# Keys, queries and FFN inputs transposed by DMA within SBUF in a chunk-selecting attention with an FFN behind it

## The chip, the cores and the metric

One Trainium2 chip, one core, one launch. The time is the device time of the launch in microseconds, as the median of several runs. A separate execution was taken with the hardware profiler; its lines are the ones that are read here, and its own time stands beside them.

## The reference

Four sequences (B) of 768 positions, eight heads of 64, float32 in and out. Keys are cut into 24 chunks of 32. For each query an upper bound of its scores with each chunk is worked out from the chunk's per-dimension minimum and maximum; the six best chunks that are not in the future are kept, and attention runs over the kept chunks with the causal mask. The result, heads side by side, is the input (3072 tokens of 512) of a two-layer FFN with a squared relu.

```
k_min, k_max = k_chunks.min(axis=3), k_chunks.max(axis=3)       # 24 chunks of 32
ub = sum_d max(q * k_min, q * k_max)                            # bound per query and chunk
top = the 6 chunks with the highest ub, future chunks left out
scores = where(chunk selected and causal, q @ k.T / 8, -1e9)
x = softmax(scores) @ v          -> (B * S, H * D) = (3072, 512)
h = relu(x @ w_in)               -> (3072, 2048)
out = (h * h) @ w_out            -> (3072, 512)
```

## The kernel before

The kernel is written as a list of operations (`plan.op`, line 60). Each has a table of engines that may do it with a planned cost in microseconds, a due number, the operations that it needs, and the buffers that it holds. `Plan.order` (line 70) simulates them greedily: of all that can start, it takes the engine with the earliest start, and among that engine's operations within 0.06 us the one with the lowest due number. The instructions are then written in order of planned start, so each engine's queue has that order for good. Hand-over times between engines are planned with `HAND_OVER`; a TensorE operation that starts before `WARM` (14.0 us) is planned at twice its cost; a load's landing is planned by its packets at 0.98 ns each, loads are issued in the order in which the program lists them, and at most eight are under way. Buffers come from pools with a fixed number of slots (`slots`), and an operation whose buffer has no free slot is planned after the one that frees it.

**Loads.** GpSimd issues all loads from HBM, casting float32 to bfloat16. The first 128 positions of all four sequences come as `firsts` (k, q) and `vfirst`, the other 640 as `nat[nm, b]` with tags `kn`, `qn`, `vn`: for sequence 0 by head pair (`load_pair`, line 321), for the others by tiles of 128 positions and all heads (`load_tile`, line 314), keys first, then queries, then values. Three sequences' worth of buffers (`B - 1`) lets the loads run far ahead. GpSimd also does some of the causal masks on the diagonal (line 578), in the same queue.

**Stage A** (`stage_a`) prepares a pair of heads (16 pairs `p`, four per sequence). Six matmuls against the identity turn the key tiles into `kT` in PSUM (`turn_keys`, line 218 by its helper), five turn the query tiles into `qT`. `kT` is copied twice into `kqs` (ScalarE line 213 or VectorE line 215) and reduced twice by VectorE to chunk maxima and minima (`kr`, line 522). `qT` is copied twice into `qss` and split by VectorE into `qp` and `qm` (line 532). TensorE forms the bounds `ub`, VectorE picks with MAX8 (line 502), and the selection is turned (`sT`) and copied below the queries in `qss`, so that the score matmul adds a large negative number to chunks not chosen.

**Stage B** (`stage_b`) does, per head, five banks of 512 scores (`ps`, line 598), the exponential on ScalarE (line 620), the diagonal mask, the products with the values (`av`, line 609) and the normalising into `x` (line 460).

**The FFN** (`ffn`) runs once for the first 128 rows of all sequences (`x_first`) and once per sequence for the other 640. `turn` transposes a tile of 128 rows by four matmuls into PSUM (`xt`) and a copy puts it into `xT`; `up` (line 678) computes 128 hidden features for a range of columns, relu on ScalarE (line 685) or VectorE (line 687) and a square on VectorE (line 696); `down` (line 708) sums over the hidden features and an output store leaves on SP's queue (line 721). For the sequences the ups go in two ranges of 320 columns, with the tiles 0 to 2 turned before the first range and 3 and 4 before the second. The FFN of sequence b is due among the attention of sequence b + 1, and the last one stands alone at the end.

SP's queue holds seven copies of constant rows at the start and the 24 output stores.

Of the kernel before, what the change touches and what calls it, by code (L numbers as in the profile page):

```python
# [11 lines left out]
AX = mybir.AxisListType  # L12
ALU = mybir.AluOpType
ACT = mybir.ActivationFunctionType
# [18 lines left out]
class Op:  # L33
    def __init__(self, where, due, fn, needs, tiles, packets):
        self.where, self.due, self.fn = where, due, fn
        self.needs, self.tiles, self.packets = needs, tiles, packets
        self.engine = None
        self.start = self.end = None


class Plan:
# [10 lines left out]
    WARM = 14.0  # L52
# [7 lines left out]
    def op(self, where, due, fn, needs=(), tiles=(), packets=0):  # L60
        op = Op(where, due, fn, [n for n in needs if n is not None],
                [t for t in tiles if t is not None], packets)
        for t in op.tiles:
            t.users.append(op)
        self.ops.append(op)
        if packets:
            self.loads.append(op)
        return op

    def order(self):  # L70
# [12 lines left out]
        while ready:  # L83
# [36 lines left out]
            op.engine, op.start, op.end = engine, st, st + cost  # L120
            free[engine] = op.end
# [30 lines left out]
def kernel(  # L152
# [9 lines left out]
    nc = tc.nc  # L162

    B, H, S, D = q.shape
    CH = 32
# [22 lines left out]
    ld = ctx.enter_context(tc.tile_pool(name="ld", bufs=B - 1))  # L188
    work = ctx.enter_context(tc.tile_pool(name="work", bufs=2))
# [9 lines left out]
                 "ob": 3, "kn": B - 1, "qn": B - 1, "vn": B - 1, "x": 2, "xT": 2,  # L199
                 "kr": 2, "qp": 2, "qm": 2, "ubm": 2, "m8": 2, "rc": 2})  # L200
    POOLS = {"tp": pst, "ps": pss, "av": psav, "ff": psf, "e": epool, "h2": hpool,
             "ht": hpool, "ob": opool, "kn": ld, "qn": ld, "vn": ld}
# [97 lines left out]
    for b in range(B):  # L300
        for nm in "kqv":
            nat[nm, b] = buffer(nm + "n", [128, NS, H, VW if nm == "v" else D])

    def ones(b, due):
        def go(engine):
            e = nc.vector if engine == "DVE" else nc.gpsimd
            e.memset(nat["v", b].tile[:, :, :, D:D + 1].rearrange(
                "p j h o -> p (j h) o"), 1.0)

        made["ones", b] = plan.op({"DVE": 0.12, "POOL": 0.3}, due, go,  # L310
                                  tiles=[nat["v", b]])

# [61 lines left out]
    for b in range(1, B):  # L374
        ones(b, 20 * NP * b - 70)
        for i, nm in enumerate("kqv"):
            for j in range(1, NT):
                load_tile(nm, b, j, 20 * NP * b - 70 + 5 * i + j)
# [90 lines left out]
    def stage_a(p):  # L469
# [4 lines left out]
        kT = buffer("tp", [128, S], name="kT")  # L474
        qT = buffer("tp" if p else "ps", [128, QC], name="qT")
# [5 lines left out]
        sT = buffer("ps", [128, NT // 2, 128], name="sT")  # L481

# [25 lines left out]
        def copy_selection(e, hh, i):  # L508
# [6 lines left out]
        t = op({"PE": 0.34}, t0, turn_keys,  # L515
               loads_of("k", b, hp) + [made["ident"]], [kT, nat["k", b]])
        late = 4 if p == 0 else 0
        kc = [op({"DVE": 0.475, "ACT": 0.74}, t0 + 3 + hh + late, lambda e, hh=hh: copy(
            e, kqs[0:D, s, hh], kT[D * hh:D * hh + D]),
            [t] + before, [kT]) for hh in range(2)]  # L520
        r = [op({"DVE": 0.86}, t0 + 5 + 2 * mm, lambda _, mm=mm, f=f:
                nc.vector.tensor_reduce(  # L522
                    kr[:, mm], kT.tile.rearrange("d (c j) -> d c j", j=CH),
                    axis=AX.X, op=f), [t], [kT, kr])
             for mm, f in ((0, ALU.max), (1, ALU.min))]
# [4 lines left out]
        t = op({"PE": 0.28}, t0 + 8, turn_queries,  # L530
               loads_of("q", b, hp, False) + [made["ident"]], [qT, nat["q", b]])
        sq = [op({"DVE": 0.40}, t0 + 10 + i, lambda _, d=d, f=f: f(  # L532
            d.tile, qT.tile, 0.0), [t], [qT, d])
            for i, (d, f) in enumerate(((qp, nc.vector.tensor_scalar_max),
                                        (qm, nc.vector.tensor_scalar_min)))]
        qc = [op({"ACT": 0.63, "DVE": 0.40}, t0 + 13 + hh, lambda e, hh=hh: copy(
            e, qss[0:D, s, hh], qT[D * hh:D * hh + D]),
            [t] + before, [qT]) for hh in range(2)]
# [100 lines left out]
    def ffn(x, ready, rows, parts, due, rate, up_tags=("ff", "ff")):  # L639

        n = len(rows)
        xT = buffer("xT", [128, NKI, 128 * n])
# [7 lines left out]
        turned = []  # L650

        def turn(t):
            pt = buffer("ff", [128, NKI, 128], name="xt")

            def go(_):
                for ki in range(NKI):
                    transpose(pt[:, ki], x[:, t, 128 * ki:128 * (ki + 1)])

            op = plan.op({"PE": 0.225}, step(0.225), go, ready(t), [pt] + xs)
            turned.append(plan.op(  # L660
                {"DVE": 0.36, "ACT": 0.54}, at[0] + 0.5,
                lambda e: copy(e, xT[:, :, 128 * t:128 * (t + 1)], pt.tile),
                [op], [pt, xT]))
# [4 lines left out]
        def up(f, c0, c1, i):  # L668
# [7 lines left out]
            def go(_):  # L676
                for ki in range(NKI):
                    nc.tensor.matmul(  # L678
                        ph.tile, lhsT=w_in_sb[:, ki, 128 * f:128 * (f + 1)],
                        rhs=xT[:, ki, c0:c1],  # L680
                        start=(ki == 0), stop=(ki == NKI - 1))

            def relu(e):
                if e == "ACT":
                    nc.scalar.activation(ht.tile, ph.tile, ACT.Relu)  # L685
                else:
# [4 lines left out]
                         turned[c0 // 128:-(-c1 // 128)] + loaded["in", f // 4],  # L691
# [43 lines left out]
    turn, up, down = ffn(x_first, lambda t: x_done[t, 0], first_rows, None,  # L735
# [13 lines left out]
    for b in range(B):  # L749
        x = buffer("x", [128, NS, d_model])  # L750
        x_done[b, 1] = []
        for p in range(NP * b, NP * (b + 1)):
# [5 lines left out]
            None, HALVES * NP * (b + 1) + 10, 2.2, ("ps", "ps") if last else ("ff", "ff"))  # L758
        for c in range(2):
            for t in ((0, 1, 2), (3, 4))[c]:  # L760
                turn(t)
            for f in range(NFI):
                up(f, QC // 2 * c, QC // 2 * (c + 1), f)
# [34 lines left out]
```

## Time and profile before

| | |
|---|---|
| median of 3 runs | 283.24 us (283.13 to 283.76) |
| the profiled execution's own time | 284.56 us |
| its span, first to last instruction | 282.8 us |
| granted TensorE clock | 1.00 |
| HBM read, written | 27.26 MB, 6.29 MB |
| GpSimd's DMA queue | 79,152 packets, 61.9% of 16 engines' span |
| SP's DMA queue | 3,708 packets, 6.3% |

How to read the profile: PE is TensorE's matmuls, PEld its weight loads, DVE VectorE, ACT ScalarE, POOL GpSimd, SP SyncE. Matmuls are pipelined, so the length of one matmul record is longer than the step from one to the next, and a busy PE is not PE at its peak. A group's line gives engine, operation, output and input tiles, shapes, count, busy time and mean length in ns, then the idle time of the engine just before and what ended it. The chain of waits is followed back from the last instruction to whatever released each step. Slices are fortieths of the span, digits are tenths. The time given for a DMA's landing is from issue to completion.

### The profile page before, as it was taken

Reading aid. Unit: us, or ns where it says so; the run is one execution under the profiler, and the core shown is the slowest. Engines: PE = TensorE matmul, PEld = TensorE weight load, DVE = VectorE, ACT = ScalarE, POOL = GpSimd, SP = SyncE. Lnnn points to the kernel's source line nnn. Section 1 sums busy time; section 2 is a strip of 40 time slices with the busy share of each in tenths; the row PEclk is TensorE's granted clock in tenths of the full one; section 3 lists DMA queues with packets and bytes.
Section 4 is the critical chain, followed back from the end, with each engine's and each line's share of the span. In section 5 each row is a group of like instructions: output and inputs, shape, how many; then the busy total and the mean of one; then the engine's idle time right before and its main releaser. Section 6 shows DMA issues by size and latency. Waiting matters only on the chain.

```text
span 282.8 us, 6701 instructions
## 1 busy us (share of the span) xinstructions
PE 265.6 (94%) x2515; PEld 174.2 (62%) x2544; DVE 209.0 (74%) x729; ACT 181.8 (64%) x348; POOL 100.3 (35%) x170
## 2 busy tenths in 40 slices
PE   6778989999999999999999999999999999899994
PEld 2555766566667776565767665667776655567441
DVE  1377999989999999676999996869999612488200
ACT  3265789997896888365868874668688544334111
POOL 8976797699999321000201211002023000000000
PEclk9999999999999999999999999999999999999999
DMA  9999999999999900011000010101000111100021
GB/s 59 183 163 190 146 126 175 178 173 178 171 166 147 81 2 37 12 64 39 37 3 3 0 39 37 41 37 39 1 3 2 38 39 54 57 2 0 37 76 74
DMA packets 82892, 20.61 MB, mean 73 GB/s; under 512 B 75524, under 2 KB 79788, under 8 KB 82860
## 3 DMA queue, kind: packets, MB, share of 16 engines
q0 software_dynamic: 79152, 13.64, 61.9%
q1 hardware_dynamic: 3708, 6.55, 6.3%
q8 instruction: 20, 0.33, 0.5%
q14 instruction: 12, 0.10, 0.1%
HBM read 27.26 MB, written 6.29 MB: 119 GB/s over the span
## 4 chain that ended last, share of the span: by engine, by line
PE 66%; DMA 11%; DVE 10%; POOL 8%; ACT 2%; issue 2%; POOLq 0%; ACTq 0%; DVEq 0%
PE py L708 24%; PE ph L678 24%; PE ps L598 8%; DMA w_out_sb<-in_moe_w_out_dram 6%; PE av L609 4%; DMA k<-in_k_dram 3%; DVE kr L522 2%; DMA qn<-in_q_dram 2%; POOL qn L314 1%; POOL qn L321 1%; POOL kn L321 1%; PE kT L218 1%; PE xt L218 1%; DVE qsc L215 1%; DVE m L502 1%
## 5 line engine op out<-in xcount | busy, mean ns | idle before, releaser
L620 ACT ACTIVATE e<-ps 128x512 bf16<-128x512 f32 x160 | 90.6, 601 | 21.7 <-PE ps L598 19.6
L678 PE MATMUL ph<-xT,w_in_sb 128*128 128x320 bf16 (+2 forms) x605 | 99.8, 303 | 1.5 <-DVE xT L215 0.5
L708 PE MATMUL py<-w_out_sb,h 128*128 128x512 bf16 x358 | 90.2, 379 | 1.2
L678 PEld LDWEIGHTS <-w_in_sb 128*128 128x128 bf16 x608 | 57.9, 98 | 26.5 <-issue 4.0
L578 POOL TENSOR_SCALAR_AFFINE_SELECT e<-e 128x128 bf16<-128x128 bf16 (+1 forms) x74 | 24.9, 339 | 126.0 <-ACT e L620 124.6
L598 PE MATMUL ps<-qsc,kqc 88*128 88x128 bf16 (+1 forms) x320 | 57.7, 272 | 0.5 <-ACT e L620 0.3
L685 ACT ACTIVATE ht<-ph 128x320 bf16<-128x320 f32 (+2 forms) x81 | 35.6, 440 | 28.9 <-PE ph L678 24.2
L708 PEld LDWEIGHTS <-h 128*128 128x128 bf16 x384 | 34.1, 97 | 30.4
L696 DVE TENSOR_TENSOR h<-ht 128x320 bf16<-128x320 bf16 (+2 forms) x152 | 46.0, 323 | 3.4 <-ACT ht L685 3.1
L609 PEld LDWEIGHTS <-e 128*128 128x128 bf16 x640 | 36.9, 97 | 12.8 <-POOL e L578 1.8
L687 DVE TENSOR_SCALAR ht<-ph 128x320 bf16<-128x320 f32 (+2 forms) x71 | 34.8, 490 | 7.0 <-PE ph L678 4.7
L609 PE MATMUL av<-vn,e 128*128 128x65 bf16 x480 | 38.6, 193 | 1.2 <-POOL e L578 0.7
L598 PEld LDWEIGHTS <-kqc 88*128 88x128 bf16 x320 | 25.6, 98 | 11.3 <-issue 1.5
L522 DVE TENSOR_REDUCE kr<-kT 128x24 bf16<-128x768 bf16 x32 | 30.1, 945 | 2.3 <-PE kT L218 2.1
L213 ACT COPY ob<-py 128x512 f32<-128x512 f32 x22 | 12.9, 588 | 27.4 <-PE py L708 27.3
L575 DVE TENSOR_TENSOR e<-e,tri 128x128 bf16<-128x128 bf16 (+1 forms) x54 | 12.8, 239 | 13.1 <-ACT e L620 12.6
L460 DVE TENSOR_TENSOR x<-av,rc 128x320 bf16<-128x320 f32 (+1 forms) x40 | 18.5, 471 | 0.4
L502 DVE MAX8 m<-ubm 128x8 f32<-128x24 f32 x160 | 15.6, 168 | 0.2
L609 PE MATMUL av<-v,e 128*128 128x65 bf16 x160 | 15.2, 193 | 0.1
L213 ACT COPY qsc<-qT 64x640 bf16<-64x640 bf16 x19 | 13.1, 687 | 1.9 <-DVE qm L532 0.7
L215 DVE COPY kqc<-kT 64x768 bf16<-64x768 bf16 x17 | 9.4, 553 | 6.6 <-PE kT L218 6.1
L314 POOL DMA_DIRECT2D qn<-in_q_dram x15 | 13.3, 896 | 2.5 <-DMA w_out_sb<-in_moe_w_out_dram 2.3
(72 smaller groups left out, 272.3 us busy)
## 6 DMA issues: line engine op xcount, KB each, us to landing
out_dram<-ob SPq DMA_DIRECT2D x24, 256.0 KB, 2.0
w_in_sb<-in_moe_w_in_dram POOLq DMA_DIRECT2D x4, 512.0 KB, 9.0
w_out_sb<-in_moe_w_out_dram POOLq DMA_DIRECT2D x4, 512.0 KB, 8.1
kn<-in_k_dram POOLq DMA_DIRECT2D x15, 128.0 KB, 6.5
qn<-in_q_dram POOLq DMA_DIRECT2D x15, 128.0 KB, 6.2
vn<-in_v_dram POOLq DMA_DIRECT2D x15, 128.0 KB, 6.1
kn<-in_k_dram POOLq DMA_DIRECT2D x8, 80.0 KB, 6.7
qn<-in_q_dram POOLq DMA_DIRECT2D x8, 80.0 KB, 6.3
```

The lines of the kernel that those rows point to most:

```text
L213: nc.scalar.copy(dst, src)
L460: return plan.op({"DVE": 0.06 + 0.00108 * D * n}, due, lambda _: nc.vector.tensor_mul(x(), av[:, :, 0:D], rc[:, 0:n].unsqueeze(2).to_broad ...
L522: nc.vector.tensor_reduce(kr[:, mm], kT.tile.rearrange("d (c j) -> d c j", j=CH), axis=AX.X, op=f), [t], [kT, kr])
L578: nc.gpsimd.affine_select(out=e, in_=e, compare_op=ALU.is_ge, fill=0.0, base=0, channel_multiplier=-1, pattern=[[0, n], [1, 128]])
L598: nc.tensor.matmul(ps[:, 128 * c:128 * (c + nt)], lhsT=kqs[:, s, hh, 128 * j:128 * (j + 1)], rhs=qss[:, s, hh, 128 * (t0 - 1):128 * (t0 - ...
L609: nc.tensor.matmul(av[:, t - 1], lhsT=e[:, 128 * c:128 * (c + 1)], rhs=value_tile(b, h, j), start=(i == 0 and c == 0), stop=(i == len(BANK ...
L620: nc.scalar.activation(e.tile, ps.tile, ACT.Exp, scale=scale), [sc], [ps, e])
L678: nc.tensor.matmul(ph.tile, lhsT=w_in_sb[:, ki, 128 * f:128 * (f + 1)], rhs=xT[:, ki, c0:c1], start=(ki == 0), stop=(ki == NKI - 1))
L685: nc.scalar.activation(ht.tile, ph.tile, ACT.Relu)
L687: nc.vector.tensor_scalar_max(ht.tile, ph.tile, 0.0)
L696: {"DVE": 0.06 + w / 1900}, at[0] + 2, lambda _: nc.vector.tensor_mul(h2[f][:, c0:c1], ht.tile, ht.tile), [op], [ht, h2[f]])))
L708: nc.tensor.matmul(py.tile, lhsT=h2[f][:, 128 * t:128 * (t + 1)], rhs=w_out_sb[:, f, :], start=(f == 0), stop=(f == NFI - 1))
```

## The change

Sequence 0 keeps its path. For the sequences 1 to 3 the key and query tiles of 128 positions are loaded by GpSimd into `nt` buffers (six slots, 128 x 512 bf16, one tile each), and SP issues for each a transposing DMA from SBUF to SBUF into `kt` or `qt` (two slots each, four pairs side by side on the free axis). The first key tile is turned the same way from `firsts`. The turns on TensorE for these sequences are gone; copies, reductions and max/min read `kt` and `qt` in SBUF and are planned on VectorE alone. A pair's keys now need the turns of all six tiles of the sequence, and its queries those of all five. The natural `kn` and `qn` buffers shrink to one, for sequence 0.

In the FFN of the sequences 0 to 2, `turn` is the same kind of DMA from `x` into `xT`; the last sequence's and the first rows' stay on TensorE. `xT` has its axes in another order. The ups of each sequence go in ranges of 256 and 384 columns, after two and three tiles.

In the planner `WARM` goes from 14.0 to 23.5, an operation may have a `lag` that delays its result but not its engine, and the costs of a few copies are other numbers. A transposing DMA is planned at 1.2 us on SP with a lag of 1.6.

```diff
-    WARM = 14.0
+    WARM = 23.5
...
-            op.engine, op.start, op.end = engine, st, st + cost
-            free[engine] = op.end
+            op.engine, op.start, op.end = engine, st, st + cost + op.lag
+            free[engine] = st + cost
...
+    ld1 = ctx.enter_context(tc.tile_pool(name="ld1", bufs=1))
+    ldt = ctx.enter_context(tc.tile_pool(name="ldt", bufs=6))
+    tpool = ctx.enter_context(tc.tile_pool(name="tpool", bufs=2))
...
-                 "ob": 3, "kn": B - 1, "qn": B - 1, "vn": B - 1, "x": 2, "xT": 2,
+                 "ob": 3, "kn": 1, "qn": 1, "nt": 6, "kt": 2, "qt": 2,
+                 "vn": B - 1, "x": 2, "xT": 2,
...
+    for b in range(1, B):
+        turned["k", b] = buffer("kt", [128, NT, NP, 128])
+        turned["q", b] = buffer("qt", [128, NS, NP, 128])
+
+    def turn_by_dma(dst, src, due, needs, tiles):
+        return plan.op({"SP": 1.2}, due, lambda _: nc.sync.dma_start_transpose(
+            out=dst(), in_=src()), needs, tiles, lag=1.6)
...
+    def load_turned(nm, b, j, due):
+        dst = turned[nm, b]
+        if j == 0:
+            src, needs = None, loaded[nm, b, "first"]
+        else:
+            src = buffer("nt", [128, H, D])
+            load((nm, b, j), lambda _: nc.gpsimd.dma_start(
+                out=src.tile,
+                in_=SRC[nm][b, :, 128 * j:128 * (j + 1)].rearrange("h p d -> p h d")),
+                due, 1024, [src])
+            needs = loaded[nm, b, j]
+        i = j if nm == "k" else j - 1
+        op = turn_by_dma(
+            lambda: dst[:, i],
+            lambda: (src.tile if src else firsts[nm][:, b]).rearrange(
+                "p h d -> p (h d)"), due, needs, [src, dst])
+        loaded.setdefault((nm, b), []).append(op)
...
-        for i, nm in enumerate("kqv"):
-            for j in range(1, NT):
-                load_tile(nm, b, j, 20 * NP * b - 70 + 5 * i + j)
+        for i, nm in enumerate("kq"):
+            for j in range(0 if nm == "k" else 1, NT):
+                load_turned(nm, b, j, 20 * NP * b - 70 + 5 * i + j)
+        for j in range(1, NT):
+            load_tile("v", b, j, 20 * NP * b - 60 + j)
...
+        if b:
+            kT, qT = turned["k", b], turned["q", b]
+        else:
+            kT = buffer("tp", [128, S], name="kT")
+            qT = buffer("tp" if p else "ps", [128, QC], name="qT")
...
+        def part(t, rows=slice(0, 128)):
+            if b:
+                return t[rows, :, hp]
+            return t[rows].rearrange("d (t j) -> d t j", j=128)
...
-        kc = [op({"DVE": 0.475, "ACT": 0.74}, t0 + 3 + hh + late, lambda e, hh=hh: copy(
-            e, kqs[0:D, s, hh], kT[D * hh:D * hh + D]),
-            [t] + before, [kT]) for hh in range(2)]
+        if b:
+            got = list(loaded["k", b])
+            kc_on, qc_on, q_on = {"DVE": 0.28}, {"DVE": 0.24}, 0.24
+        else:
+            got = [op({"PE": 0.34}, t0, turn_keys, loads_of("k", b, hp) + [made["ident"]],
+                      [kT, nat["k", b]])]
+            kc_on, qc_on = {"DVE": 0.475, "ACT": 0.80}, {"ACT": 0.69, "DVE": 0.41}
+            q_on = 0.40
+        kc = [op(kc_on, t0 + 3 + hh + late, lambda e, hh=hh: copy(
+            e, by_tile(kqs[0:D, s, hh]), part(kT, slice(D * hh, D * hh + D))),
+            got + before, [kT]) for hh in range(2)]
...
-        t = op({"PE": 0.28}, t0 + 8, turn_queries,
-               loads_of("q", b, hp, False) + [made["ident"]], [qT, nat["q", b]])
+        if b:
+            got = list(loaded["q", b])
+        else:
+            got = [op({"PE": 0.28}, t0 + 8, turn_queries,
+                      loads_of("q", b, hp, False) + [made["ident"]], [qT, nat["q", b]])]
...
-        xT = buffer("xT", [128, NKI, 128 * n])
+        xT = buffer("xT", [128, n, NKI, 128])
...
         def turn(t):
+            if by_dma:
+                xt_made.append(turn_by_dma(
+                    lambda: xT[:, t], lambda: x[:, t], step(0.225), ready(t),
+                    [xT] + xs))
+                return
...
-            None, HALVES * NP * (b + 1) + 10, 2.2, ("ps", "ps") if last else ("ff", "ff"))
+            not last, HALVES * NP * (b + 1) + 10, 2.2, ("ps", "ps") if last else ("ff", "ff"))
         for c in range(2):
-            for t in ((0, 1, 2), (3, 4))[c]:
+            tiles = range(2 * c, 2 + (NS - 2) * c)
+            for t in tiles:
                 turn(t)
             for f in range(NFI):
-                up(f, QC // 2 * c, QC // 2 * (c + 1), f)
+                up(f, 128 * tiles[0], 128 * (tiles[-1] + 1), f)
```

## The prediction

> **What bounds the kernel now.** I read the page's busy table and slices first, then the windows by stretch, then the chain of waits, the groups by form, and last GpSimd's timeline and the landing times.
>
> ```profile
> PE 265.6 (94%) x2515; PEld 174.2 (62%) x2544; DVE 209.0 (74%) x729; ACT 181.8 (64%) x348; POOL 100.3 (35%) x170
> DMA  9999999999999900011000010101000111100021
> PE 66%; DMA 11%; DVE 10%; POOL 8%; ACT 2%; issue 2%; POOLq 0%; ACTq 0%; DVEq 0%
> ```
>
> TensorE is busy 94% of the span and carries two thirds of the chain; the DMA engines are full to about 99 us (14 of 40 slices of 7.07 us) and almost idle after. By stretch (columns: length, then PE, PEld, DVE, ACT, POOL busy, granted clock, DMA):
>
> ```profile
> 0.00:20.00 20.00, 13.99 (x99) 8.32 (x100) 8.23 (x31) 8.23 (x12) 17.34 (x25) 1.00 1.68 133
> 20.00:40.00 20.00, 17.86 (x181) 13.31 (x181) 16.67 (x67) 13.22 (x29) 15.26 (x23) 1.00 1.52 155
> 60.00:100.00 40.00, 39.11 (x447) 27.55 (x450) 38.22 (x132) 32.81 (x65) 33.02 (x47) 1.00 1.98 148
> 100.00:140.00 40.00, 39.24 (x403) 25.46 (x404) 31.85 (x110) 28.15 (x54) 4.82 (x15) 1.00 0.09 34
> 140.00:190.00 50.00, 48.85 (x480) 32.47 (x486) 42.51 (x151) 34.21 (x65) 6.81 (x20) 1.00 0.06 23
> 190.00:240.00 50.00, 49.21 (x485) 32.98 (x488) 35.35 (x119) 34.29 (x67) 7.05 (x21) 1.00 0.06 23
> ```
>
> From 60 to 240 us PE is busy 176.4 of 180 us, 98%; its gaps lie before 40 us. Busy is not peak, so I count issue steps from the chain (start, length, what):
>
> ```profile
> 112.52 1.09 PE ph L678 x8
> 118.89 0.86 PE py L708 x4
> 134.60 0.45 PE xt L218 x8
> ```
>
> An FFN column costs 1.09/8/320 = 0.426 ns, a transpose 0.45/8 = 0.056 us. All of PE: FFN 2 x 196,608 columns x 0.423 ns = 166 us; scores 81,920 x 0.425 = 35; 352 transposes x 0.056 = 20; 672 value products x 0.03 = 20; bounds 4; first attention and warm-up 7: 252 of 282.8 us. Of the other 31, about 18 lie before 40 us. From 60 us on PE is the bound; DVE, 96% in 60 to 100, is close behind it there.
>
> **PE transposes removed.** Pairs of sequences 1 to 3: 12 x (6 key + 5 query tiles) = 132. FFN inputs of sequences 0 to 2: 15 x 4 = 60. Together 192 x 0.056 = 10.75 us, all of it between 59.85 us (first key transposes of sequence 1) and 212 us. At 98%: **-10.5 us**. The Trainium skill, page "TensorE: Matmul & The Clock Gate", section "Part 4: PE-mode transpose", puts one transpose at about 275 ns inside a kernel; that would make this 52.8 us. The trace's own record of one is 219 ns long, but eight take 0.45 us: the lengths overlap and only the step comes back.
>
> **Copies.** Per pair, the key and query copies move from PSUM sources on either engine to SBUF sources on VectorE alone:
>
> ```profile
> L215 DVE COPY kqc<-kT 64x768 bf16<-64x768 bf16 x17 | 9.4, 553 | 6.6 <-PE kT L218 6.1
> L213 ACT COPY qsc<-qT 64x640 bf16<-64x640 bf16 x19 | 13.1, 687 | 1.9 <-DVE qm L532 0.7
> L532 DVE TENSOR_SCALAR qp<-qT 128x640 bf16<-128x640 bf16 x16 | 7.8, 485 | 1.0 <-PE qT L218 0.8
> L215 DVE COPY xT<-xt 128x512 bf16<-128x512 bf16 x12 | 4.9, 412 | 3.9 <-PE xt L218 3.8
> ```
>
> ScalarE loses 15/16 x 0.79 + 19/16 x 0.687 = 1.56 us a pair, 18.7 in all, and about 4 of xT. VectorE has 17/16 x 0.553 + 13/16 x 0.483 = 0.98 of copies and 0.97 of max/min a pair. With SBUF sources no row shows these. Lower end: 0.196 (tri from ahead, SBUF to SBUF, 128x128); upper end: today's 0.553 and 0.483. The squaring h<-ht, 128x320 with two SBUF operands at 0.322 against 0.485 for relu from PSUM, is nearest, so I take the change's own plan figures plus the 0.08 by which the trace exceeds the plan today (0.553 against 0.475): 0.36 and 0.32. Then 2 x 0.36 + 4 x 0.32 = 2.0 against 1.95: VectorE gains nothing a pair and loses the xT copies, 3 us. The path gets **0**: PE covers it, and without that cover the upper end is the third rival.
>
> **What SP gains.** 48 transposing DMAs of 128x512: 18 key, 15 query, 15 input tiles. The trace has none. Nearest rows: SP's SBUF-to-SBUF copies of 36 KB, 0.76 us from issue to issue; output stores of 256 KB,
>
> ```profile
> DMA to landing us min/median/max: 2.0/2.0/5.6
> ```
>
> 2.0 us in quiet, 5.6 for the one seen in the full stretch (issued at 59.5); and GpSimd's 128 KB loads, 6.1 to 6.5 us. So an issue costs 0.3 (a store's) to 2 us and a landing 2.0 to 6.5; I take 1.2 an issue (the plan's figure, inside the bounds) and 2.8 in quiet, 5.6 in the full stretch. SP is then occupied 48 x 1.2 = 58 of 280 us. Queued behind a transpose that waits for its tile are output stores (three `ob` buffers, so PE's down results wait only if a store is some 4 us late) and the next transposes.
>
> Against the change stands the Trainium skill, page "VectorE: DVE Perf Modes", section "The three transpose paths": 1309 ns for 128x128 by the DMA crossbar against 390 by TensorE, with the advice to use TensorE where PSUM will do. Four blocks one after the other would be 5.2 us a tile, 251 us for 48, and the slower rival would hold. The trace answers for PE's side, 0.056 us a block, and has no row for the other.
>
> **Sequence 1's start.** This is where the added wait bites:
>
> ```profile
> 45.56 4.41 POOL L314 DMA_DIRECT2D kn<-in_k_dram  x5
> 50.08 0.88 POOL L314 DMA_DIRECT2D qn<-in_q_dram  x1
> 57.14 0.90 POOL L314 DMA_DIRECT2D qn<-in_q_dram  x1
> L218 PE MATMUL qT<-ident,qn x5: 219/219/219, 65.8 to 66.0; 128*128 128x128 bf16 x5
> ```
>
> Today the last query tile is issued at 57.1, lands by about 63.5 and is turned at 65.8; the pair's selection is copied by 73.2 and its scores start at about 75. After: keys land at 52 to 56. The six `nt` slots hold k1 to k5 and q1, so q2 is issued when k1 is turned (52 + 5.6, near 58, today 52.6), q5 near 61; it lands at 67.5 and is turned at 72 to 73. Prepared 7 us later, at 79 to 80: some 4 to 5 late. GpSimd's diagonal masks stand behind the waiting load. Cover: of the first rows' `py` work two groups of 0.86 are left after 76.5 us, and sequence 0's FFN, whose inputs are ready at 75.9, can't start before them (next part). Bounds 0 and +5; I take **+3**, the delay less those two groups. Later sequences have over 20 us in hand.
>
> **FFN inputs.** Normalised at 75.9 and 130.1, first `ph` at 82.1 and about 136.7. Two issues and a landing: 75.9 + 1.2 + 5.6 = 82.7; 130.1 + 1.2 + 2.8 = 134.1. At 134 PE still has `py` and attention to do; at 82 the +3 above already pays for its lack of work: **0** (0 to +1).
>
> **Split 256/384 for 320/320.** Equal columns and counts; relu 0.423 (256) and 0.485 (320) lie on one line: 0. The last FFN, still on PE, starts after two tiles, not three; its first `ph` follows 1.2 us of idle around `xt` at 242 to 244: **-0.5** (0 to -1.3).
>
> **Plan.** WARM 23.5 doubles PE's price up to 23.5 us in the planner, so the order before 40 us changes. The first matmuls are paced by loads (GpSimd 17.3 of 20 us busy): **0**, plus or minus 1. ScalarE's relief and fewer small PE waits could give 0 to -2; taken as 0.
>
> **Sum** against the profiled execution, 284.56 us (span 282.8 and 1.76 around it): 284.56 - 10.5 - 0.5 + 3 = 276.6. The median of the runs, 283.24, is 1.32 lower: 275.2 us. All good ends: 283.24 - 10.5 - 1.3 - 2 - 1 = 268.4. All bad ends: 283.24 - 10.5 + 5 + 1 + 1 = 279.7.
>
> **Rivals.** (1) Slower: the transposing DMA is serial on SP, at s us a tile. Sequence 1's 11 tiles start at 52, so its first pair is ready at 52 + 11s + 7, against 75 needed and 2 us of cover. The gains of 11 us are used up where 52 + 11s + 7 = 75 + 2 + 11, s = 2.6; at s = 4 it is ready at 103, 26 us uncovered, minus 11: 298 us. Beyond 54/16 = 3.4 a sequence's 16 tiles no longer fit its period of some 54 us. For it: engines that are full to 99 us, and 5.6 us for a store. Against: stores at 2.0 in quiet, plain copies at 0.76. (2) Sequence 1 is late by all 5 us, and late FFN inputs and loads behind `nt` on GpSimd add 2 to 3: 278 to 282, say 280. For it: POOL busy 33 of 40 us there. Against: PE's `py` groups. (3) VectorE becomes the bound: if SBUF copies cost as from PSUM, it pays 2 x 0.553 + 4 x 0.483 = 3.04 a pair for 1.95, +13 in all, -3 of xT. In about half of 60 to 240 VectorE is over 93% busy (by stretches of 10 us): +5 there, and in the other half PE gives -5.2; with -0.5 and +3, 285.5. The h row speaks against it.
>
> **Chances.** The sum's case 0.60, rival 2 0.16, rival 3 0.05, rival 1 0.19. A measurement of this kernel can tell about 0.2%, 0.6 us, from no change. Rivals 3 and 1 hold nearly all of slower (0.21) and the no-change case gets 0.03 from the seams: faster 0.76. The range runs from 268.5, the good ends, to 285, which leaves out most of rival 1 and a little of the rest.
>
> **What would show it.** Transposes on `kT`, `qT`, `xt` fall from 272 to 80; 48 transposing DMAs on SP, 1.2 us apart at least, landing in 2.8 us after 100 us and near 5.6 before; the first query maxima of sequence 1 at 72 to 74, not 66.3; PE busy still 97% or more from 100 us on; the last `x` near 230, not 239. Wrong would be: PE idle by microseconds with SP or a DMA as releaser past 100 us, landings over 4 us in quiet, or VectorE copies near 0.5.

## The result: slower by 5.6%, and the profile after

| | before | after |
|---|---|---|
| median of the runs | 283.5 us (4 runs, 283.13 to 284.35) | 299.87 us (4 runs, 297.24 to 301.0) |
| ratio | | 1.056 (95%: 1.048 to 1.064) |
| the profiled execution's own time, span | 284.56, 282.8 us | 301.0, 299.3 us |
| granted TensorE clock over the span | 1.00 | 0.948 |

The forecast was 275.2 us with a range up to 285.0; the median lies 14.9 us above its end. All comparisons below are of medians on the same chip; a number such as "+9.2" is the difference of the two medians in us. The ratios go by the means of the runs, so they can differ a little from the quotient of the medians. The clock's 1.00 before is a little flattering: other executions of the kernel before list 0.98 to 1.00, and the last section shows that its first 20 us were not at full clock.

The page of the changed kernel first: busy time, then slices of 7.5 us, then the chain's shares by engine.

```profile
PE 261.4 (87%) x2329; PEld 165.2 (55%) x2352; DVE 205.0 (69%) x726; ACT 170.4 (57%) x333; POOL 101.5 (34%) x173
...
PEclk9859999977999978999996999999999999999999
DMA  8999999999999999994122000113300011100011
...
PE 43%; DMA 22%; DVE 18%; POOL 9%; issue 3%; SPq 2%; ACT 1%; POOLq 0%; DVEq 0%; ACTq 0%
```

TensorE still does most, but its share of the chain fell from 66% to 43%; DMA and VectorE took it over, and in several slices up to 165 us the granted clock is below full. The span grew by 16.5 us. TensorE's busy time fell by 4.2 us (265.6 to 261.4), so its idle time grew by 20.7 (17.2 to 37.9). Of the 10.75 us of transposes taken out, 6.5 came back as longer busy time. The DMA engines are full for the first 18 slices, to about 135 us; before they were to 99. The last load is issued at 128.6 us, 92.3 before. The stretches (columns as in the prediction: length, busy PE, PEld, DVE, ACT, POOL, granted clock, DMA) show where:

```profile
20.00:40.00 20.00, 17.81 (x201) 13.31 (x199) 16.38 (x68) 14.61 (x33) 15.18 (x23) 0.94 1.78 173
60.00:100.00 40.00, 29.00 (x275) 17.81 (x277) 28.21 (x98) 18.39 (x37) 27.03 (x37) 0.91 1.78 158
100.00:140.00 40.00, 32.40 (x282) 20.04 (x284) 32.90 (x110) 20.98 (x42) 16.78 (x29) 0.91 1.48 123
140.00:190.00 50.00, 46.56 (x429) 30.66 (x431) 45.55 (x153) 32.68 (x65) 6.52 (x20) 0.93 0.11 31
190.00:240.00 50.00, 49.73 (x496) 33.14 (x500) 36.73 (x142) 34.48 (x69) 6.60 (x21) 1.00 0.14 41
...
66.00:68.00 2.00, 2.00 (x11) 1.08 (x10) 0.13 (x1) 0.21 (x1) 2.00 (x3) 0.50 2.31 150
156.00:162.00 6.00, 5.47 (x32) 3.83 (x31) 4.15 (x13) 2.99 (x7) 0.99 (x3) 0.50 0.45 109
```

Between 60 and 140 us TensorE was busy 78.4 of 80 us; now it is busy 61.4, at a lower clock. From 190 to 240 us it is 99.5% busy at full clock: there the change works as meant. The loss thus lies at the start of sequence 1 and in what comes behind it. The chain of waits in that stretch (start, length, what):

```profile
44.05 11.00 DMA nt<-in_k_dram
55.07 1.19 SPq L317
56.35 5.58 DMA kt<-nt
62.02 0.49 POOL nt L335
64.79 0.30 POOL e L635
70.25 8.70 DMA nt<-in_k_dram
78.97 6.55 DMA kt<-nt
90.60 6.53 DMA nt<-in_q_dram
100.13 2.78 SPq L317
102.95 7.80 DMA xT<-x
110.89 1.12 PE ph L739 x3
```

The first key tile lands at 55.05, not 52; turns land and free `nt` slots only by 61.94; GpSimd issues the next query tile at 62.02, and a mask (`e`) stands behind the loads. SP turns ten tiles one after the other, as its timeline shows (start, length of the whole group; the third line is the second line's group without its first turn):

```profile
55.07 7.07 SPq L317 DMA_TRANSPOSE kt<-nt  x5
62.23 9.58 SPq L317 DMA_TRANSPOSE qt<-nt  x5
66.55 5.26 SPq L317 DMA_TRANSPOSE qt<-nt  x4
...
81.81 4.46 SPq L317 DMA_TRANSPOSE kt<-nt  x3
86.55 2.50 SPq L317 DMA_TRANSPOSE xT<-x  x2
89.14 1.28 SPq L317 DMA_TRANSPOSE kt<-nt  x1
...
91.14 7.24 SPq L317 DMA_TRANSPOSE qt<-nt  x5
98.44 5.84 SPq L317 DMA_TRANSPOSE xT<-x  x3
```

Ten turns take 55.07 to 71.81, 1.67 us each on average. In this kernel 3.1 of these us are SP's wait for the second query tile: the first one's turn is issued by 63.45, the next starts at 66.55. The landing times (the last column of the profile's list of DMA issues) are medians of the few landings that the trace tells, seven of the 48:

```profile
kt<-nt SPq DMA_TRANSPOSE x15, 4.8
qt<-nt SPq DMA_TRANSPOSE x15, 6.8
xT<-x SPq DMA_TRANSPOSE x15, 2.4
kt<-k SPq DMA_TRANSPOSE x3, 8.5
```

The first query maxima of sequence 1 come at 78.2 (66.3 before; 72 to 74 was forecast). Further down SP's queue, turns of sequence 2 stand between the tiles of `x`: its five turns begin at 86.55 and end at 104.28. What TensorE does meanwhile, from its timeline (the bracket is the idle time before and its releaser):

```profile
60.91 0.38 PE L655 MATMUL ps<-qsc,kqc 88*128 88x128 bf16 x2
65.16 0.40 PE L666 MATMUL av<-vn,e 128*128 128x65 bf16 x4 [3.87 <-POOL e L635]
65.36 1.90 PE L769 MATMUL py<-w_out_sb,h 128*128 128x512 bf16 x4
...
106.32 0.81 PE L769 MATMUL py<-w_out_sb,h 128*128 128x512 bf16 x3
110.89 1.44 PE L739 MATMUL ph<-xT,w_in_sb 128*128 128x384 bf16 x4 [3.76 <-DMA xT<-x]
```

Behind the first wait four `py` take 1.90 us; the record of four at full clock is 1.03. The clock was 0.50 from 64 to 70 us (the last window above is part of it), and 0.76 in 110 to 120, behind the second wait. The Trainium skill, page "TensorE: Matmul & The Clock Gate", section "Part 1: The HAM clock gate", states that TensorE goes back to half clock after an idle window of about 3.4 us. The two waits, 3.87 and 3.76 us, are of that length, but the clock column falls sooner: at about 63.5, 2.2 us into the first, and within the first us of the second (0.50 from 108 on). It was also 0.50 from 156 to 162 us, behind a wait of only 1.78 us at 153.2, and in the kernel with sequence 1 alone (below) from 63.5 to 66.5, behind one of 2.96. So here the clock fell without a single wait of that length before it.

VectorE's copies, by form (count, busy, mean ns, idle before):

```profile
L220 DVE COPY kqc<-kt 64x768 bf16<-64x768 bf16 x24 | 8.9, 370 | 2.5 <-DMA kt<-nt 2.3
L220 DVE COPY qsc<-qt 64x640 bf16<-64x640 bf16 x24 | 11.4, 477 | 0.2
L589 DVE TENSOR_SCALAR qp<-qt 128x640 bf16<-128x640 bf16 x12 | 5.7, 473 | 3.5 <-issue 3.5
```

The key copies got cheaper (0.553 to 0.370), the query copies and maxima did not.

### The profile page after: what moved, and what is told of

It is laid out like the page before. It is cut to its first block, busy times and chain, and to the rows that moved or that the text cites. A ratio compares the mean times of both kernels' runs of the same rounds, so it can differ in the third digit from the quotient of the medians.

```text
span 299.3 us, 6453 instructions
## 1 busy us (share of the span) xinstructions
PE 261.4 (87%) x2329; PEld 165.2 (55%) x2352; DVE 205.0 (69%) x726; ACT 170.4 (57%) x333; POOL 101.5 (34%) x173
## 4 chain that ended last, share of the span: by engine, by line
PE 43%; DMA 22%; DVE 18%; POOL 9%; issue 3%; SPq 2%; ACT 1%; POOLq 0%; DVEq 0%; ACTq 0%
PE py L769 17%; PE ph L739 16%; DMA nt<-in_k_dram 7%; PE ps L655 5%; DVE kr L575 4%; DMA kt<-nt 4%; DMA kn<-in_k_dram 4%; DMA k<-in_k_dram 3%; PE av L666 3%; DVE h L757 3%; DMA xT<-x 3%; DVE qsc L220 2%; SPq L317 2%; DMA nt<-in_q_dram 2%; DVE ht L748 2%
## 5 line engine op out<-in xcount | busy, mean ns | idle before, releaser
L739 PE MATMUL ph<-xT,w_in_sb 128*128 128x256 bf16 (+2 forms) x608 | 103.5, 309 | 7.5 <-DMA xT<-x 3.8
L769 PE MATMUL py<-w_out_sb,h 128*128 128x512 bf16 x361 | 93.3, 384 | 1.8 <-ACT xT L218 0.5
L746 ACT ACTIVATE ht<-ph 128x384 bf16<-128x384 f32 (+2 forms) x98 | 44.0, 450 | 41.1 <-PE ph L739 32.4
L655 PE MATMUL ps<-qsc,kqc 88*128 88x128 bf16 (+1 forms) x320 | 61.2, 280 | 0.7 <-ACT e L677 0.3
L757 DVE TENSOR_TENSOR h<-ht 128x256 bf16<-128x256 bf16 (+2 forms) x152 | 47.3, 321 | 16.8 <-ACT ht L746 15.9
L748 DVE TENSOR_SCALAR ht<-ph 128x256 bf16<-128x256 f32 (+2 forms) x54 | 25.1, 468 | 4.2 <-PE ph L739 3.6
L575 DVE TENSOR_REDUCE kr<-kt 128x24 bf16<-128x768 bf16 x24 | 22.0, 943 | 0.2
L335 POOL DMA_DIRECT2D nt<-in_q_dram x15 | 13.5, 902 | 11.4 <-DMA kt<-nt 10.0
L335 POOL DMA_DIRECT2D nt<-in_k_dram x15 | 13.4, 918 | 3.9 <-DMA qt<-nt 3.4
L220 DVE COPY qsc<-sT 24x256 bf16<-24x256 bf16 (+1 forms) x36 | 11.4, 318 | 4.6 <-PE sT L223 3.9
```

The costliest lines, as they stand in the source:

```text
L335: load((nm, b, j), lambda _: nc.gpsimd.dma_start(out=src.tile, in_=SRC[nm][b, :, 128 * j:128 * (j + 1)].rearrange("h p d -> p h d")), due, ...
L575: nc.vector.tensor_reduce(kr[:, mm].rearrange("d (t c) -> d t c", c=128 // CH), part(kT).rearrange("d t (c j) -> d t c j", j=CH), axis=AX. ...
L655: nc.tensor.matmul(ps[:, 128 * c:128 * (c + nt)], lhsT=kqs[:, s, hh, 128 * j:128 * (j + 1)], rhs=qss[:, s, hh, 128 * (t0 - 1):128 * (t0 - ...
L739: nc.tensor.matmul(ph.tile, lhsT=w_in_sb[:, ki, 128 * f:128 * (f + 1)], rhs=xT[:, c0 // 128:c1 // 128, ki], start=(ki == 0), stop=(ki == N ...
L748: nc.vector.tensor_scalar_max(ht.tile, ph.tile, 0.0)
L757: {"DVE": 0.06 + w / 1900}, at[0] + 2, lambda _: nc.vector.tensor_mul(h2[f][:, c0:c1], ht.tile, ht.tile), [op], [ht, h2[f]])))
```

## The experiments

The theory after the comparison: sequence 1's start is late because SP turns its tiles in series from a late first landing, and the lateness costs TensorE idle time and clock. The rivals: the `nt` slots hold GpSimd back; GpSimd's masks behind the waiting load; VectorE, which alone may copy now; the FFN inputs; the planner's numbers. All kernels but the first are the changed kernel with the edit shown, and so have `WARM` 23.5 and the ranges 256 and 384; where a sequence goes back to TensorE its natural buffers come back too. Where sequence 1 alone goes by DMA, one `kt` and at most one `qt` slot are left.

**The parts, each alone.** The planner's number, in the kernel before:

```diff
-    WARM = 14.0
+    WARM = 23.5
```

> The kernel before with WARM 23.5 instead of 14.0 and nothing else. Theory A (GpSimd's loads wait for nt slots that a late turn frees, the diagonal masks stand behind them in GpSimd's queue, TensorE idles and its clock falls) and theory B (the turned tiles themselves land too late among the loads, whatever the slots): 282 to 285 us. Theory C (the order that the planner now writes is the worse one): 290 us or more, with PE idle before 60 us.

Measured: 282.94 against 283.83, ratio 0.9965 (0.9948 to 0.9982), -0.9 us. The plan's number is not the loss; it brings a little.

Only the FFN inputs of sequences 0 to 2 (the keys and queries of all sequences on TensorE):

```diff
+    KQ = 4   # sequences from KQ on by DMA: none
-        if b:
+        if b >= KQ:
```

> The change with keys and queries of all sequences on TensorE as before; only the FFN inputs of sequences 0 to 2 are turned by DMA (60 transposes off PE, 3.4 us). Theories A and B: 279 to 283 us, granted clock back at 1.00. If the FFN inputs on SP were a main cost: 290 us or more with PE waiting for xT.

The same, with sequence 0's inputs on TensorE too:

```diff
-            not last, HALVES * NP * (b + 1) + 10, 2.2, ...
+            b in (1, 2), HALVES * NP * (b + 1) + 10, 2.2, ...
```

> Only the FFN inputs of sequences 1 and 2 by DMA (40 transposes off PE, 2.2 us), in the stretch without loads; all keys and queries on TensorE. Theory B: 280 to 282.5 us and no wait of PE on xT. If a turn by DMA costs the path even with quiet engines: 283.5 to 286 us, as with the inputs of all three.

Measured: 284.99 against 283.83, 1.0054 (1.0021 to 1.0086), and 281.93 against 283.77, 0.995 (0.992 to 0.998): +1.2 and -1.8. Sequence 0's five tiles alone make the difference of 3 us, though they take 1.1 us of transposes away. The timeline of TensorE in the first of these two shows the place:

```profile
80.75 1.03 PE L772 MATMUL py<-w_out_sb,h 128*128 128x512 bf16 x4
84.61 0.61 PE L742 MATMUL ph<-xT,w_in_sb 128*128 128x256 bf16 x4 [2.83 <-DMA xT<-x]
```

It waits 2.83 us for the transposing DMA before the FFN of sequence 0, in the stretch in which the loads run.

Only the keys and queries of sequences 1 to 3, then those of sequence 1 alone, then of sequence 1 only the keys:

```diff
-            not last, HALVES * NP * (b + 1) + 10, 2.2, ...
+            b in (), HALVES * NP * (b + 1) + 10, 2.2, ...
...
+    BY_DMA = (1,)   # second and third kernel; all FFN inputs on TensorE in all three
-        if b:
+        if b in BY_DMA:
...
-            got = list(loaded["q", b])  # third: queries turned on TensorE
```

> The change with all FFN inputs on TensorE; only keys and queries of sequences 1 to 3 are turned by DMA (132 transposes off PE, 7.4 us). Theories A and B: 295 to 302 us, nearly the whole loss, with clock below 1 from 60 to 130 us. If the loss needs both halves, because inputs and tiles share SP's queue: below 288 us.

> Only the keys and queries of sequence 1 by DMA; those of 2 and 3 and all FFN inputs on TensorE (44 transposes off PE, 2.5 us). Theory B (sequence 1's tiles come late because SP turns them one after the other from 55 us on and each lands 5 to 8 us later): most of the loss of the keys-and-queries half is here, 289 to 294 us. If the loss is spread over the sequences alike: 284 to 288 us.

> Of sequence 1 the keys alone by DMA, queries on TensorE; all else as before. SP then has 6 turns instead of 11 before the first pair can go on, and the query tiles need no slot. Theory B with SP's serial turning as the cause: the chunk bounds come by 73 to 74 us instead of 78, and the time is 284 to 288 us. If the first landing alone decides: 290 us or more.

| by DMA | ratio (95%) | us |
|---|---|---|
| keys, queries of 1 to 3 | 1.0378 (1.0353 to 1.0403) | +10.7 |
| keys, queries of 1 | 1.0304 (1.0258 to 1.0351) | +9.2 |
| keys of 1 | 1.019 (1.0157 to 1.0222) | +5.3 |

One sequence carries most of the loss. The windows of 60 to 100 us and the query maxima (count, shortest, middle and longest ns, first and last start), first for keys and queries of sequence 1, then for its keys alone:

```profile
60.00:100.00 40.00, 30.94 (x315) 20.00 (x314) 30.32 (x102) 20.03 (x39) 30.07 (x42) 0.96 1.78 147
L593 DVE TENSOR_SCALAR qp<-qt x2: 475/480/486, 77.5 to 80.4; 128x640 bf16<-128x640 bf16 x2
```

```profile
60.00:100.00 40.00, 34.93 (x371) 23.39 (x370) 32.21 (x115) 25.91 (x52) 24.80 (x40) 0.96 1.62 127
L593 DVE TENSOR_SCALAR qp<-qT x2: 468/470/471, 72.3 to 78.2; 128x640 bf16<-128x640 bf16 x2
```

With five turns fewer on SP the first query maxima of sequence 1 start at 72.3 instead of 77.5, TensorE is busy 4 us more of these 40, and the kernel loses 3.9 us less. Of these 5.2 us, 1.8 are an earlier first turn (53.65 against 55.43), and the query tiles need no `nt` slot here either; the next kernel looks at the slots.

**What makes sequence 1 late.** More slots, so that GpSimd needn't wait:

```diff
-    ldt = ctx.enter_context(tc.tile_pool(name="ldt", bufs=6))
+    ldt = ctx.enter_context(tc.tile_pool(name="ldt", bufs=10))
...
-                 "ob": 3, "kn": 1, "qn": 1, "nt": 6, "kt": 2, "qt": 2,
+                 "ob": 3, "kn": 1, "qn": 1, "nt": 10, "kt": 2, "qt": 2,
```

> The change with ten nt slots instead of six, so that the ten key and query tiles of a sequence never wait for a turn of their own sequence. Theory A: q2 to q5 of sequence 1 are issued by 53 us, not 62 to 65, GpSimd does not stop for 10 us, and the time falls to 277 to 287 us. Theory B: landings stay at 5 to 8 us, the first pair of sequence 1 is as late as before, and the time stays at 294 to 301 us.

Measured: 298.17 against 283.83, 1.052 (1.0474 to 1.0567): +14.3, no gain clear of the noise. The timeline of GpSimd has the query loads early again, as in the kernel before, and the tile's view has the turns and their landing:

```profile
56.75 0.90 POOL L335 DMA_DIRECT2D nt<-in_q_dram  x1
```

```profile
L589 DVE TENSOR_SCALAR qp<-qt x12: 448/478/486, 77.7 to 204.2; 128x640 bf16<-128x640 bf16 x12
L317 SPq DMA_TRANSPOSE qt<-nt x15: 1200/1431/3007, 62.4 to 125.4; - x15
...
DMA to landing us min/median/max: 3.9/7.1/7.6
```

The last of these loads is issued at 56.75, yet the first maxima come at 77.7 instead of 78.2: the turns of the queries start at 62.4 as in the changed kernel, take up to 3.0 us each, and land 7.1 us after issue. That load lands 11.9 us after its issue; the same load took 6.2 us before, so turns and loads also slow each other. How much of the lateness that is was not isolated. The slots alone are not what makes sequence 1 late: without their waits, the turns in series and their landings make it as late.

Masks on VectorE only, so that none stands behind a waiting load on GpSimd:

```diff
-                        {"DVE": 0.085 + 0.058 * n, "POOL": 0.15 + 0.13 * n}, due + 1.5,
+                        {"DVE": 0.085 + 0.058 * n}, due + 1.5,
```

> The change with all diagonal masks of the sequences planned on VectorE, none on GpSimd, so that nothing on the way to the values stands behind a load that waits for a slot. Theory A: the 4 us gap of PE at 61 us and those after it vanish and the time is 284 to 291 us. Theory B: the first pair of sequence 1 is as late as before, its query maxima at 77 us or later, and the time is 294 to 301 us.

Measured: 297.95 against 283.77, 1.052 (1.0446 to 1.0594). That mask is the releaser that the trace names for the wait of 3.87 us; without it there the time is much the same, as TensorE waits 6.5 us for the bounds (`ub`) at 72 us instead. Ten slots and the masks on VectorE together were not tried.

A planned landing nearer to the measured one:

```diff
-            out=dst(), in_=src()), needs, tiles, lag=1.6)
+            out=dst(), in_=src()), needs, tiles, lag=5.5)
```

> The change with the planner's lag of a turn 5.5 us instead of 1.6, near the 4.8 to 6.8 us measured among the loads; nothing else. If the order written for early turns is the cause (PE's queue holds work that waits for turns, with other work behind it): 285 to 291 us. Theory B in its strict form (the tiles are late, and there is not enough other work): 293 us or more.

Measured: 295.23 against 283.77, 1.0414 (1.0357 to 1.0472), +11.5 instead of +16.4. The order written for too early a landing costs some 5 us, which may be the same as those of the next part; the rest stays.

**What comes behind the lateness.** The copies of keys and queries allowed on ScalarE again, with the planned prices of VectorE's query copies and maxima raised to 0.40; then, in the plan alone, a pair prepared only after the first scores of the pair two before it (in the changed kernel VectorE's and SP's free time lets the planner pull it ahead); then both:

```diff
-            kc_on, qc_on, q_on = {"DVE": 0.28}, {"DVE": 0.24}, 0.24
+            kc_on, qc_on, q_on = {"DVE": 0.28, "ACT": 0.80}, {"DVE": 0.40, "ACT": 0.69}, 0.40
...
-            got = list(loaded["k", b])
+            got = list(loaded["k", b]) + scored.get(p - 2, [])[:1]
...
-            got = list(loaded["q", b])
+            got = list(loaded["q", b]) + scored.get(p - 2, [])[:1]
```

> The change with the copies of turned keys and queries open to ScalarE too, at the costs that the kernel before measured there, and with 0.40 us for query copies and maxima on VectorE, which is near the 0.47 measured. Theory D (VectorE, given all copies, is full from 120 to 150 us while ScalarE is half idle, and TensorE runs out of prepared pairs): 288 to 294 us. Theory B: 296 to 301 us.

> The change, but the planner may prepare a pair of the sequences 1 to 3 only once the scores of the pair two before have begun; before the change the single kT/qT buffer in PSUM held the pairs apart. Theory E (with all tiles of a sequence turned at once, VectorE prepares pairs far ahead of their due time and delays masks, squares and normalising of the pair in hand): 286 to 293 us. Theories B and D: 296 to 301 us.

> The whole change with both edits, ScalarE copies and held-back preparation. If the two are separate terms beside sequence 1's lateness: 286 to 290 us. If they are the same term seen twice: 292 to 295 us. Theory B says that it stays above 285 in any case.

And both with only sequence 1's keys and queries by DMA:

> Sequence 1's keys and queries alone by DMA, with ScalarE allowed for their copies and early preparation held back. Theory B, lateness alone: 289 to 293 us, as without these two edits. If VectorE's load or the order was the cost there too: 284 to 287 us.

| kernel | ratio (95%) | us |
|---|---|---|
| the change | 1.056 (1.0478 to 1.0642) | +16.4 |
| with ScalarE's copies and the prices | 1.0333 (1.029 to 1.0376) | +9.6 |
| with the order held back | 1.0371 (1.0336 to 1.0406) | +10.5 |
| with both | 1.023 (1.0183 to 1.0278) | +6.8 |
| only sequence 1, with both | 1.0208 (1.0174 to 1.0242) | +6.2 |

They take 6.8 and some 6 us off, both together 9.6: in part the same term. VectorE is the likely one: in the kernel with keys and queries alone it is full from 100 to 140 us (31.85 of 40 before), and TensorE is not:

```profile
100.00:140.00 40.00, 35.87 (x317) 21.60 (x319) 38.82 (x114) 25.02 (x52) 16.13 (x28) 1.00 1.32 114
```

How the 9.6 us share out between VectorE's time and the order was not isolated. Sequence 1 alone loses 3.0 us less with both (+9.2 to +6.2). What neither edit takes away of the whole change, +6.8, is about as large as that.

**Where the turns have time.** Sequence 0's and 1's keys and queries and sequence 0's FFN inputs stay on TensorE, the rest goes by DMA (value buffers two, not three, for space):

```diff
+    KQ = 2
-        if b:
+        if b >= KQ:
...
-                 "vn": B - 1, "x": 2, "xT": 2,
+                 "vn": 2, "x": 2, "xT": 2,
```

> The change, but sequence 1 keeps its keys and queries on TensorE and sequence 0 its FFN inputs; by DMA go the keys and queries of sequences 2 and 3 and the FFN inputs of 1 and 2 (88 + 40 transposes off PE, 7.2 us). For room the v buffers are two, not three. Theory B (a turned tile is late because SP issues one in 1.2 us or more and it lands 5 to 8 us later among the loads, which only the first pair of sequence 1 and the inputs of sequence 0 can't bear): 276 to 281 us, faster than before. Theory A (GpSimd's waits on nt slots hold up the masks wherever loads and turns meet): 286 to 294 us, as the loads of sequences 2 and 3 wait for slots here too.

Measured: 295.33 against 283.77, 1.04 (1.0347 to 1.0453). This one is confounded: with two value buffers the values of sequence 3 load at 138 to 143 us beside the turns of `x`, and TensorE waits 5.0 us for `xT`; nor was the order held back. The next kernels keep three value buffers, have one `kt` and `qt` slot, and the order held back. Sequence 3 and the FFN inputs of 1 and 2; sequence 2 alone; sequences 2 and 3 and the FFN inputs; and the first again with ScalarE's copies:

```diff
+    BY_DMA = (3,)     # then (2,), (2, 3), (3,)
-            not last, HALVES * NP * (b + 1) + 10, 2.2, ...
+            b in (1, 2), HALVES * NP * (b + 1) + 10, 2.2, ...   # none for (2,)
```

> By DMA only what has time: keys and queries of sequence 3 (44 transposes) and FFN inputs of sequences 1 and 2 (40), with the same hold on early preparation; all else on TensorE. 84 transposes off PE, 4.7 us. Theories B and E: 278 to 281 us. Theory D, or if turns by DMA cost in quiet too: 283 us or more.

> Keys and queries of sequence 2 alone by DMA, preparation held back; 44 transposes off PE, 2.5 us. If only lateness costs: 280 to 282 us, as sequence 2 has over 30 us between its loads and its first pair. If loads that wait for slots hold up GpSimd's masks wherever turns meet loads: 283 to 286 us.

> Keys and queries of sequences 2 and 3 and FFN inputs of 1 and 2 by DMA, preparation held back, one kt and one qt slot, so that sequence 3 is turned when 2 is prepared. 88 + 40 transposes off PE, 7.2 us. Theory B with sequence 1 as the place of the loss: 276 to 280 us. If each sequence by DMA costs: 283 us or more.

> The faster version (sequence 3's keys and queries, inputs of sequences 1 and 2 by DMA), with ScalarE allowed for the copies. If VectorE is short there too: 277 to 279 us. If PE alone bounds that stretch: 279 to 280.5 us, no change.

| by DMA | transposes taken off TensorE | ratio (95%) | us |
|---|---|---|---|
| 3, FFN 1 and 2 | 84, 4.7 us | 0.9871 (0.982 to 0.9921) | -4.0 |
| 2 | 44, 2.5 us | 0.9983 (0.995 to 1.0016) | -1.2 |
| 2, 3, FFN 1 and 2 | 128, 7.2 us | 1.001 (0.9984 to 1.0037) | 0.0 |
| 3, FFN 1 and 2, ScalarE | 84, 4.7 us | 0.9859 (0.9784 to 0.9933) | -4.9 |

The first and the last beat both kernels; they are not told apart. The windows of the first show what the change looks like where nothing is late:

```profile
60.00:100.00 40.00, 39.18 (x447) 27.55 (x445) 37.87 (x129) 32.72 (x63) 32.96 (x50) 1.00 2.07 164
100.00:140.00 40.00, 39.34 (x376) 25.20 (x375) 31.68 (x108) 27.52 (x52) 4.18 (x14) 1.00 0.40 64
```

TensorE stays at 98% and full clock though SP turns ten tiles of sequence 3 from 81.9 to 98.4 in the same full stretch: nobody waits for them until 157. Sequence 2 alone gains nothing measurable beyond the planner's 0.9 (by the means it is -0.5), though 2.5 us are off TensorE. Its window shows where they went:

```profile
60.00:100.00 40.00, 37.45 (x414) 26.43 (x417) 36.38 (x125) 31.15 (x61) 30.30 (x45) 1.00 2.06 158
```

TensorE was busy 39.11 us there before. GpSimd waits 4.5 us for a turn of sequence 2 to free an `nt` slot, a mask of sequence 1 stands behind the load, and TensorE waits 1.53 us for the mask: the slots, which alone did not explain sequence 1, do cost here. Two sequences through one `kt` and `qt` slot come out even: TensorE is busy only 7.92 of 10 us from 170 to 180, where sequence 3's first pairs are due, and GpSimd waits 5.9 us in all for `nt` slots. Which of the two takes the gain was not tested.

Seven of the measured times lie in none of the ranges expected of them: the one with two value buffers above both, and six between the two (the FFN inputs of 0 to 2, keys and queries alone, keys of 1, the order held back, both edits, sequence 2). A range went with one cause acting alone.

## Why the prediction was wrong, step by step

**Transposes removed, -10.5.** Two thirds of it came where nothing was late: 4.7 us taken off gave -4.0, of which 0.9 is the plan's number. In the change as a whole it does not show.

**The last FFN after two tiles, -0.5.** Not seen: from the last `x` to the end it is 43.8 us before (239.0 to 282.8) and 44.3 after (255.0 to 299.3).

**Sequence 1's start, +3 (0 to +5): the step that failed.** Sequence 1 alone costs +9.2 with 2.5 us of transposes gone, so its price is 11.7; with ScalarE's copies and the order held back it is 8.7, still outside the bounds. The mechanism was named, its terms were too small, and the last link was missing:
- The first landing: 55.05, at the late end of the "52 to 56" of the text, which then went on with 52. The 52 is the issue at 45.56 and the 6.5 us of other loads. The five key tiles of sequence 1 landed later than that even in the kernel before, the first at about 55.7, as its view shows:

```profile
DMA to landing us min/median/max: 10.0/10.1/10.1
```

- The chain: I followed one query tile from slot to slot. Each link came later: slots free at 61.9 (58 in the text), the fifth query tile issued at 65.0 (61), landed at 70.4 (67.5), its turn issued at 70.5, first maxima at 78.2 (72 to 74). The ten turns in series, which the text left out, end at the same time: 55.1 + 10 x 1.67 = 71.8. With ten slots the slot links are gone, and the series alone again ends at 71.9 and gives 77.7. With my 1.2 and 5.6 the tenth turn would have been issued at 52 + 9 x 1.2 = 62.8 and landed at 68.4, so it did not show.
- The price of lateness: I took off two groups of `py` as cover and let each us late cost one us at most. The start is 11.9 us late, and behind its waits TensorE also ran at half clock. That the clock gives back most of the 6.5 us of longer busy time is worked out from the records; no run isolates it.

**"Later sequences have over 20 us in hand."** Their tiles did, but not the engines. Adding sequences 2 and 3 to sequence 1 should have given -4.9 and gave +1.5 (+9.2 to +10.7). Their copies were taken ahead: the fourth pair of sequence 2 has its query maxima at 145.8, against 163.1 with sequence 1 alone by DMA, while VectorE is full. Holding the order back and ScalarE's copies took 9.6 us off the whole change, some 3 of them at sequence 1.

**Copies, 0.** VectorE's relief was overstated: key copies 0.370 as assumed (0.36), query copies 0.477 and maxima 0.473 where 0.32 was assumed. Per pair 2 x 0.370 + 2 x 0.477 + 0.473 + 0.470 = 2.64 us instead of 2.0. "PE covers it" held where nothing was late: there ScalarE's help made no difference that could be told (-4.9 against -4.0). In the changed kernel that help, with the raised prices, was worth 6.8 us.

The Trainium skill, page "VectorE: DVE Perf Modes", section "Rules for kernel authors", gives a dense bf16 copy from SBUF to SBUF as four times the base rate, and one from PSUM as the base rate; here the key copy went from 0.553 to 0.370, and the query copy of 0.477 gained nothing, so neither comes near a factor of four.

**FFN inputs, 0 (0 to +1).** For sequences 1 and 2 right: landings of 2.4 in the changed kernel and 3.8 in the kernel with these alone, one or two told in each (2.8 assumed), and a gain of 1.8. For sequence 0 wrong: the 3.0 us between the two kernels, with 1.1 us of transposes forgone, put its price at some 4.

**SP's issue and the quiet landing.** 1.2 and 2.8 were good (1.2 to 1.3, and 2.4 to 3.8 without loads beside them). Under load the landings told were 4.8 to 8.5 by tile, not 5.6, and single issues took up to 3.0.

**The plan, 0 plus or minus 1.** -0.9 in the kernel before: inside. In the changed kernel its `lag` of 1.6 cost some 5.

**The rivals.** The first, the serial transposing on SP, had the right place and sign, but its condition (2.6 us a tile) did not hold: 1.67, waits included, was enough, since it started at 52 and left out the landing. By its own sum with the measured terms (the tenth turn issued at 70.5, its landing 6.8, the pair 7) the pair is ready at 84.3 against 77, so 7.3 us late; the price was 8.7 to 11.7. The second had the mishaps but let them cost only 278 to 282. The third was half right: query copies as dear as from PSUM, and VectorE full from 120 to 150 us (29.57 of 30), of which TensorE lacks work only in the first 10.

From the kernel of sequence 1 alone on, the ladder is: +9.2, with sequences 2 and 3 +10.7, with the FFN inputs +16.4. The last step is larger than the FFN inputs alone (+1.2). SP's queue carries both, and the second wait of TensorE, 3.76 us, is for an `x` tile behind turns of sequence 2. How the 5.7 us of that step share out was not tested. Beyond the forecast these are 8.7 us for sequence 1 (11.7 less the 3 forecast), 6.4 for sequences 2 and 3 (1.5 and the 4.9 that did not show) and 9.1 for the FFN inputs (5.7 and 3.4 that did not show): 24.2 of the 24.7 us between the forecast and the median.

## What to carry to other kernels

Work moved from a full engine to a queue is worth its time only where nobody waits for it: price the whole series on the new queue, with landings as long as loads beside it make them, and give each us of lateness on the first consumer its follow-up costs. Moving the keys and queries of sequence 3, with tens of us between landing and use, and the FFN inputs of two sequences outside the loads gave -4.0 us; moving all gave +16.4. After such a move look at what the scheduler pulls ahead into the engines that it believes free.

## What the runs showed of the hardware that was not expected

- A transposing DMA of 128x512 bf16 from SBUF to SBUF kept SP 1.2 us and landed in 2.4 to 2.5 us in quiet in the changed kernel (3.8 in that of the FFN inputs of sequences 1 and 2); beside GpSimd's loads the landings told in the changed kernel were 4.8 to 8.5 us. The Trainium skill's 1309 ns for one 128x128 block ("VectorE: DVE Perf Modes", "The three transpose paths") would be, as an estimate, 5.2 us for the four blocks of a tile; the quiet landings here are shorter.
- Copies of 64x640 from `qt` took 0.477 us and of 64x768 from `kt` 0.370, both bf16 in SBUF. Five blocks of 128 against six is the difference that the code shows; why the smaller is slower stays open.
- The clock column of the profile can be wrong. It gives the first 20 us 0.81 in the changed kernel and 1.00 before. But from 12 to 23 us of the kernel before the 128x128 transposes of `k` are 307 ns long, as in the changed kernel in the stretch at 0.52 (308); from 30 to 40 us they are 218. So TensorE was slow there in both, and the start does not explain the loss.
